# Batch 0 of a fused attention and MLP kernel: unpadded scores, gathered global rows, spare matmuls and a new order of work

## Chip, cores, metric

One core of one Trainium2 chip runs the whole program. The metric is device time in microseconds (us) of one execution, the median of several; lower is better. In one call (a set of kernels run in turn, in the same rounds) the executions of the kernel before lie within 0.2 to 0.7% of each other.

## What is computed

Eight batches of attention over 576 tokens, 8 heads of 64, with a window of 32 tokens to each side and 8 global tokens; then a residual token mixer and a channel MLP with a hidden width of 2048.

```python
mask = (abs(pos[:, None] - pos[None, :]) <= 32) | is_global[:, None] | is_global[None, :]
attn = softmax(where(mask, q @ k.T / 8, -1e9))
x = (attn @ v).transpose(0, 2, 1, 3).reshape(8, 576, 512)

a1 = alpha1 * x + beta1
u = x + lam * einsum("ts,bsd->btd", w_tok, a1)     # token mix
a2 = alpha2 * u + beta2
out = u + lam * (relu(a2 @ w_ch1) @ w_ch2)         # channel MLP
```

## The kernel before

After batch 0 the kernel is one stream of nine groups of MLP matmuls on TensorE, with the attention of the next batch woven in between them. Batch 0 has no MLP to hide behind. Its work is written as a list of short names, the schedule `FIRST`; each name issues a few instructions, and each engine runs its own in the order of the list. `x:3` means that x gets PSUM bank 3.

```python
FIRST = """
i1 kgz qz1 ktz qz0 gb1 pgz gbm:0 gbc cq0 ck0 OH tk0:1 ar1 vez tq0:2 kt0 cq1 ck1 ptz qa0 tq1:3 qb0 tk1:4 qa1
qb1 Vi cq2 ck2 ar2 tq2:5 kt1 tk2:6 qa2 ck3 tt:7 kt2 cq3 kq1 gl0:0 ktt qtt tq3:1 ge0 qb2 gl2:2 qb3 qa3 wi s01:3
...
ad3 we5 tx3:5 W1s ut3 beta1
"""
```

`tk`, `tq` transpose K and Q; `s` are the scores and `e` their exp; `pt`, `pg` multiply them by the mask; `pvx`, `pvy` are probabilities times V; `nx`, `ny` divide by the row sums; `xl` multiplies by alpha1 and lambda; `tm` mixes the tokens; `tx`, `ut` make the MLP's input; `W1s` starts the MLP.

The parts that the change and the argument touch:

```python
    # odd 128-row chunks of V, shifted by 64 rows: two copies by DMA, SBUF to SBUF
    def copy_vo(b):
        ve, vo = Ve[b % 2], Vo[b % 2]
        nc.sync.dma_start(out=vo[0:64], in_=ve[64:128, 0:4])
        nc.sync.dma_start(out=vo[64:128], in_=ve[0:64, 1:5])

    # two heads in one matmul: Q padded with zeros for the other head
    def sc_mm(ps, b, hp, u):
        off = 0
        for t in (3 * u, 3 * u + 1, 3 * u + 2):
            n = 72 if t % 2 == 0 else 64
            mm(ps[:, off : off + 2 * n].rearrange(...), KT[b % 2][:, hp, 64 * t : 64 * t + P], QP[:, hp, :, t, 0:n], True, True)
            off += 2 * n

    # rows of the global tokens picked by one-hot matmuls (batches 0 and 1)
    def glob_mm(ps, b, hp, n):
        for i in range(n):
            for m, st_ in enumerate((KB0, QB0[b])):
                o = ps[:, 16 * i + 8 * m : 16 * i + 8 * m + 8]
                for j in range(4):
                    mm(o, quad(st_, hp + i, j), OH[:, j, :], j == 0, False)
                mm(o, TSB[:, 128 * (hp + i) : 128 * (hp + i) + 128], OH[:, 4 + m, :], False, True)
    ...
    # constants: all issued at the start
    for t_, src in ((LA1, alpha1), (LAM, lam)):
        nc.sync.dma_start(out=t_, in_=src.unsqueeze(0).to_broadcast([P, DM]))
    for r in (64, 0):
        nc.sync.dma_start(out=LB[r : r + 1, :], in_=beta1.unsqueeze(0))
    nc.sync.dma_start(out=abr[0:4, :], in_=beta2.rearrange("(c p) -> c p", p=P))
    nc.sync.dma_start(out=abr[4:8, :], in_=alpha2.rearrange("(c p) -> c p", p=P))
    ...
    nc.sync.dma_start(out=A2, in_=alpha2.unsqueeze(0).to_broadcast([P, DM]))
```

The softmax here doesn't subtract the row's maximum and nothing guards it: scores larger than these inputs give would overflow.

Of the kernel before, what the change touches and what calls it, by code (L numbers as in the profile page):

```python
# [18 lines left out]
D = 64  # L19
# [26 lines left out]
i1 kgz qz1 ktz qz0 gb1 pgz gbm:0 gbc cq0 ck0 OH tk0:1 ar1 vez tq0:2 kt0 cq1 ck1 ptz qa0 tq1:3 qb0 tk1:4 qa1  # L46
qb1 Vi cq2 ck2 ar2 tq2:5 kt1 tk2:6 qa2 ck3 tt:7 kt2 cq3 kq1 gl0:0 ktt qtt tq3:1 ge0 qb2 gl2:2 qb3 qa3 wi s01:3
GM gl1:4 e01 tk3:6 s00:7 ge1 kt3 s02:5 e02 ge2 ab:0 s11:1 s12:3 e00 s10:4 abe gk1:6 e12 pgc mask e11 pt0 gk0:5
e10 fz eg1 pg1 pg0 eg0 q1:2 pt1 s21:7 ra1 s22:0 b1i q0:3 e21 G s20:1 ra0 s31:4 e20 s30:6 rd0 s32:5 e22 beta
pvx0:7 e31 pg2 pvy0:3 nx0 e32 wt2:1 e30 wt1:0 ny0 we2 pg3 q2:4 wt3:5 we1 pt2 q3:7 ra2 we3 wt4:6 LA1 rd2 ra3  # L50
wt0:3 xm0 we4 rd1 pvx2:1 rd3 we0 pvx1:0 xl0 nx2 pvy1:5 pvy2:4 nx1 xl2 rs:2 pt3 xl1 ny2 pvx3:7 re rf ny1 xm2
pvy3:6 tm0:3 ny3 xm1 v1 xm3 tm2:4 ad0 nx3 tm1:5 ru:2 rv ad2 xl3 tx0:6 ad1 tx2:3 ut0 tx1:7 ut2 tm3:4 ut1 wt5:1
ad3 we5 tx3:5 W1s ut3 beta1
# [4 lines left out]
def _consts():  # L58
# [19 lines left out]
    c32[:, 40:44] = 4 * p[:, None] + np.arange(4)[None, :]  # L78
    c32[:, 44] = np.where(p < 64, 512 + p, -1)
    c32[:, 45] = np.where(p >= 64, 448 + p, -1)  # L80
# [22 lines left out]
def kernel(ctx, tc, q, k, v, global_idx, alpha1, beta1, w_tok, alpha2, beta2, w_ch1, w_ch2, lam, out):  # L103
# [34 lines left out]
    OH = T("OH", [P, 6, 8], BF16)  # L138
# [56 lines left out]

    KST = XR[:, 4:8, :].rearrange("p a b -> p (a b)").rearrange("p (h j d) -> p h j d", h=H, j=4)
    QST = XR[:, 8:12, :].rearrange("p a b -> p (a b)").rearrange("p (h j d) -> p h j d", h=H, j=4)
    WTB = HTt[:, 0 : 5 * S].rearrange("p (c s) -> p c s", c=5)
# [50 lines left out]
    def gather_x(i):  # L249
        for a in range(2):  # L250
            nc.vector.tensor_scalar(out=KQX[i][:, a, :], in0=KQG[i], scalar1=C32[:, 30 + a : 31 + a], scalar2=None, op0=ALU.mult)
# [32 lines left out]

    def gk_ev(ps, q0, n):
        nc.scalar.activation(out=EG[:, q0 : q0 + n], in_=ps[:, 0:n], func=AF.Exp, bias=0.0, scale=0.125)
# [12 lines left out]
    def probs_q(hp):  # L299
        e, pg = E[hp % 2], PGQ[hp]  # L300
        p1 = e.ap[0]
        gq_in = bass.AP(e.tensor, e.offset + 64, [p1, [272, 5], [72, 2], [1, 8]])
        gq_m = bass.AP(gqm.tensor, gqm.offset, [gqm.ap[0], [8, 5], [0, 2], [1, 8]])
        for c0 in (64, 96):
            nc.vector.tensor_tensor(out=pg[:, :, c0 : c0 + 16].rearrange("p c (a g) -> p c a g", a=2), in0=gq_in, in1=gq_m, op=ALU.mult)  # L305

    def probs_k(hp):
        e, pt = E[hp % 2], PT[hp % 2]
        p0, p1 = pt.ap[0], e.ap[0]
        for par, n in ((0, 5), (1, 4)):  # L310
            w = 72 if par == 0 else 64
            nc.vector.tensor_tensor(  # L312
                out=bass.AP(pt.tensor, pt.offset + 64 + 128 * par, [p0, [256, n], [1216, 2], [1, 64]]),
                in0=bass.AP(e.tensor, e.offset + 144 * par, [p1, [272, n], [w, 2], [1, 64]]),
# [17 lines left out]
    def sc_exp(ps, hp, u):  # L332
        n = UOFF[u + 1] - UOFF[u]
        nc.scalar.activation(out=E[hp % 2][:, UOFF[u] : UOFF[u + 1]], in_=ps[:, 0:n], func=AF.Exp, bias=0.0, scale=0.125)  # L334

    def sc_unit(b, hp, u):
        def f():
            ps = sc_ps()
            sc_mm(ps, b, hp, u)
            sc_exp(ps, hp, u)  # L340
            if u == 2:
                probs_q(hp)
                probs_k(hp)
# [25 lines left out]
    def pv_mms(b, hp, i, o):  # L369
        par = b % 2  # L370
        gs = slice(128 * i, 128 * i + 128) if i < 4 else (slice(576, 704) if par == 0 else slice(512, 640))
        pt = PT[hp % 2]
# [24 lines left out]
    def xl_eng(b, hp):  # L397
        return nc.vector if (b, hp) in ((0, 3),) else nc.gpsimd
# [16 lines left out]
    def norm_y(ps, b, hp):  # L415
# [3 lines left out]
        norm(ps, rt, 1, 1, r0, r0 + 64, SR[r0 : r0 + 64, (b // 2) % 2, cs].rearrange("p (i a d) -> p i a d", i=1, a=2))  # L419

# [50 lines left out]
    def tok_tile(b, i):  # L471
        par = b % 2

        def f():
            ps = pv_ps()
            cs = slice(64 + 128 * i, 192 + 128 * i)
# [7 lines left out]
    def tok_shared(p):  # L484
        def f():
            ps = pv_ps()
            for s in range(5):
                for par in range(2):
                    l = wt4o[:, 0:64] if s == 4 and par == 1 else wtT[:, s, 0:64]
# [113 lines left out]
    def pair_q(ps, hp, a, copy):  # L603
        ps, r = ps.bitcast(BF16), slice(64 * a, 64 * a + 64)
        copy(
            out=QP[r, hp, a, 0:8, 0:64].rearrange("p t (u j) -> p t u j", j=4),
            in_=ps[r, 0:512].rearrange("p (j t u) -> p t u j", j=4, t=8),
        )

    def tr_pair(b, hp):  # L610
        def f():
# [4 lines left out]
            for a in range(2):  # L616
                pair_q(psq, hp, a, nc.vector.tensor_copy)
# [17 lines left out]

    def tr_tail(b):
# [8 lines left out]
    def glob_mm(ps, b, hp, n):  # L645
        for i in range(n):
            for m, st_ in enumerate((KB0, QB0[b])):
                o = ps[:, 16 * i + 8 * m : 16 * i + 8 * m + 8]
                for j in range(4):
                    mm(o, quad(st_, hp + i, j), OH[:, j, :], j == 0, False)  # L650
                mm(o, TSB[:, 128 * (hp + i) : 128 * (hp + i) + 128], OH[:, 4 + m, :], False, True)

    def glob_ev(ps, hp, n):
        v_ = ps[:, 0 : 16 * n].rearrange("p (i m) -> p i m", m=16)
        for a in range(2):
            r = slice(64 * a, 64 * a + 64)
            k0 = KGP[r, hp, 16 * hp + 8 * a : 16 * hp + 8 * a + 8]
            nc.vector.tensor_copy(out=bass.AP(KGP.tensor, k0.offset, [k0.ap[0], [P + 16, n], [1, 8]]), in_=v_[r, :, 0:8])
            q_, d0 = v_[r, :, 8:16], QP[r, hp, a, 0, 64:72]
            nc.vector.tensor_copy(  # L660
                out=bass.AP(QP.tensor, d0.offset, [d0.ap[0], [2 * NW * 72, n], [144, 5], [1, 8]]),
                in_=bass.AP(q_.tensor, q_.offset, [q_.ap[0], [16, n], [0, 5], [1, 8]]),
            )

    def glob(b, hp):
        def f():
            ps = pv_ps()
            glob_mm(ps, b, hp, 1)
# [413 lines left out]
```

## Time and profile before

| | before |
|---|---|
| time, median of three (range) | 401.21 us (400.45 to 403.22) |
| span of the profiled run | 398.0 us |
| first MLP matmul | 45.97 us |
| scores begin | 14.9 us |
| TensorE idle before the first MLP matmul | 11.6 of 46 us |

The profile is of another execution, of 399.87 us. The span is some 2 us shorter than the time of the same run. The first MLP matmul is where batch 0 hands over to the stream; the prediction calls it T0, and so does this document. T0 says what batch 0 costs, and the span minus T0 says what the rest costs. The lines for all this are in the prediction.

### The profile page before, as it was taken

The page shows a single profiled execution, that of the slowest core. Times are in us where ns is not written, and L with a number is a line of the kernel's source. Part 1 is how long each engine was busy: PE and PEld are TensorE (multiplying, and loading weights), DVE is VectorE, ACT ScalarE, POOL GpSimd, SP SyncE. Part 2 cuts the span into 40 slices and gives each one's busy share as a digit, 9 for nine tenths or more (in the row PEclk, how much of TensorE's full clock was granted, in tenths as well). Part 3 has the DMA queues.
Part 4 walks back from the last instruction along what each step waited for, and adds up shares of the span by engine and source line. Part 5 has one row for each costly group of instructions (what it writes and reads, how often), then busy time and mean ns, then how long its engine had stood idle before and what let it go on. Part 6 is the DMA issues. An engine that isn't in the chain of part 4 may idle for free.

```text
span 398.0 us, 8191 instructions
## 1 busy us (share of the span) xinstructions
PE 376.7 (95%) x3088; PEld 213.5 (54%) x3141; DVE 228.8 (57%) x615; ACT 169.0 (42%) x322; POOL 212.8 (53%) x282
## 2 busy tenths in 40 slices
PE   6668989998999999999999999999999999999996
PEld 3557666554664466546654665466546654444443
DVE  5657786876457656774578467754775564114023
ACT  4644577201870186008700870088108800640720
POOL 8925987447946883687367936874350335000000
PEclk9988999999999999999999999999999999999999
DMA  9999999986998999799959995999331004102002
GB/s 247 196 241 253 216 149 141 127 139 113 153 153 123 153 145 133 101 117 170 130 107 148 134 147 107 140 143 150 94 94 40 2 28 98 49 1 79 28 26 79
DMA packets 161628, 48.68 MB, mean 122 GB/s; under 512 B 147324, under 2 KB 154564, under 8 KB 161590
## 3 DMA queue, kind: packets, MB, share of 16 engines
q0 software_dynamic: 99840, 17.19, 66.0%
q1 hardware_dynamic: 60662, 29.93, 38.8%
q10 hardware_dynamic: 1088, 1.05, 0.8%
q8 instruction: 24, 0.39, 0.4%
q14 instruction: 14, 0.11, 0.1%
HBM read 39.31 MB, written 9.44 MB: 122 GB/s over the span
## 4 chain that ended last, share of the span: by engine, by line
PE 85%; POOL 5%; DVE 4%; DMA 3%; issue 2%; ACT 0%; SPq 0%; POOLq 0%
PE bank L130 84%; DMA Vo<-Ve 2%; POOL Ve L213 1%; PE bank L813 1%; DMA UT<-UB 1%; DVE XR L543 1%; DVE XR L841 1%; DVE OT L542 1%; DVE XR L395 0%; PE bank L595 0%; POOL PGQ L570 0%; POOL Ve L570 0%; DVE PT L312 0%; POOL W L701 0%; POOL PGQ L789 0%
## 5 line engine op out<-in xcount | busy, mean ns | idle before, releaser
L130 PE MATMUL bank<-UT,W 128*128 128x512 bf16 x546 | 152.8, 379 | 2.5 <-DMA UT<-UB 1.1
L130 PE MATMUL bank<-W,HT 128*128 128x512 bf16 (+2 forms) x572 | 138.0, 373 | 1.0 <-issue 0.2
L527 ACT ACTIVATE HT<-bank,bias 128x512 bf16<-128x512 f32 x128 | 87.8, 687 | 52.6 <-PE bank L130 51.8
L334 ACT ACTIVATE E<-bank 128x416 f16<-128x416 f32 (+1 forms) x96 | 47.2, 515 | 122.3 <-PE bank L130 121.5
L130 PEld LDWEIGHTS <-HT 128*128 128x128 bf16 x592 | 53.3, 98 | 52.7 <-issue 1.6
L413 POOL TENSOR_TENSOR XL<-XR,LA 128x384 bf16<-128x384 f32 x31 | 31.3, 1012 | 75.3 <-DVE XR L395 53.8
L130 PEld LDWEIGHTS <-W 128*128 128x128 bf16 x640 | 50.7, 97 | 28.0 <-issue 2.1
L542 DVE TENSOR_TENSOR OT<-bank,LAM 128x512 f32<-128x512 f32 (+2 forms) x37 | 24.9, 674 | 54.8 <-PE bank L130 54.6
L468 POOL TENSOR_TENSOR UB<-XR,A 128x512 bf16<-128x512 f32 x28 | 35.8, 1288 | 23.7 <-DVE XR L463 15.8
L130 PEld LDWEIGHTS <-PT 128*128 128x128 f16 x576 | 33.5, 99 | 22.7 <-DMA Vo<-Ve 3.8
L130 PE MATMUL bank<-RG,G 128*128 128x65 f16 x320 | 43.9, 194 | 1.0 <-DVE RG L356 0.6
L130 PE MATMUL bank<-Ve,PT 128*128 128x65 f16 x320 | 44.0, 196 | 0.1
L130 PE MATMUL bank<-XL,wtT 128*128 128x512 bf16 (+2 forms) x238 | 41.1, 326 | 0.1
L130 PE MATMUL bank<-Vo,PT 128*128 128x65 f16 x256 | 35.6, 194 | 4.6 <-DMA Vo<-Ve 3.6
L130 PEld LDWEIGHTS <-G 128*128 128x128 f16 x320 | 31.2, 98 | 14.3
L213 POOL DMA_DIRECT2D Ve<-in_v_dram x40 | 34.1, 868 | 2.9 <-PE bank L130 2.5
L130 PEld LDWEIGHTS <-KT 128*128 128x128 bf16 x288 | 24.5, 100 | 17.8 <-issue 1.3
L130 PE MATMUL bank<-QP,KT 128*128 128x144 bf16 (+1 forms) x288 | 33.0, 228 | 0.9 <-DVE QP L660 0.6
L395 DVE TENSOR_TENSOR XR<-bank,rd 128x384 f32<-128x384 f32 (+1 forms) x64 | 27.2, 425 | 2.3
L543 DVE TENSOR_TENSOR XR<-OT,XR 128x512 f32<-128x512 f32 (+2 forms) x33 | 27.2, 825 | 1.6
L130 PEld LDWEIGHTS <-wtT 128*128 128x128 bf16 (+1 forms) x240 | 18.6, 99 | 17.6 <-issue 1.7
L305 DVE TENSOR_TENSOR PGQ<-E,gqm 128x80 f16<-128x80 f16 x64 | 10.2, 201 | 30.7 <-ACT E L334 29.5
(137 smaller groups left out, 426.4 us busy)
## 6 DMA issues: line engine op xcount, KB each, us to landing
out_dram<-XR SPq DMA_DIRECT2D x31, 256.0 KB, 2.0
Vo<-Ve SPq DMA_DIRECT2D x16, 260.0 KB, 5.4
W<-in_moe_w_ch_dram POOLq DMA_DIRECT2D x4, 1024.0 KB, 24.3
Ve<-in_v_dram POOLq DMA_DIRECT2D x24, 128.0 KB, 6.7
Kb<-in_k_dram POOLq DMA_DIRECT2D x24, 128.0 KB, 5.2
Qb<-in_q_dram POOLq DMA_DIRECT2D x24, 128.0 KB, 6.2
Ve<-in_v_dram POOLq DMA_DIRECT2D x16, 96.0 KB, 3.8
XR<-in_q_dram ACTq DMA_DIRECT2D x4, 256.0 KB, 3.9
```

The costliest lines, as they stand in the source:

```text
L130: nc.tensor.matmul(out=o, lhsT=l, rhs=r, start=st, stop=sp, skip_group_check=True)
L213: nc.gpsimd.dma_start(out=Ve[b % 2][r0 : r0 + hi - lo, c, :, 0:D], in_=v[b, :, lo:hi, :].rearrange("h p d -> p h d"))
L305: nc.vector.tensor_tensor(out=pg[:, :, c0 : c0 + 16].rearrange("p c (a g) -> p c a g", a=2), in0=gq_in, in1=gq_m, op=ALU.mult)
L334: nc.scalar.activation(out=E[hp % 2][:, UOFF[u] : UOFF[u + 1]], in_=ps[:, 0:n], func=AF.Exp, bias=0.0, scale=0.125)
L395: nc.vector.tensor_tensor(out=xo, in0=pv[:, :, :, 0:64], in1=rb, op=ALU.mult)
L413: xl_eng(b, hp).tensor_tensor(out=XL[b % 2][:, 0:3, cs], in0=XR[:, base : base + 3, cs], in1=lb, op=ALU.mult)
L468: nc.gpsimd.tensor_tensor(out=ub, in0=x, in1=A2, op=ALU.mult)
L527: nc.scalar.activation(out=HT[:, ec, :], in_=st[ec], func=AF.Relu, bias=b_, scale=1.0)
L542: nc.vector.tensor_tensor(out=ot, in0=ps, in1=LAM[:, lo:hi], op=ALU.mult)
L543: nc.vector.tensor_tensor(out=x, in0=ot, in1=x, op=ALU.add)
L813: nc.tensor.transpose(out=ps[0:n, 64 + 128 * t : 192 + 128 * t], in_=WTB[:, t, cols], identity=identb)
L841: nc.vector.tensor_tensor(out=x, in0=ps.rearrange("p (i c) -> p i c", i=4), in1=x, op=ALU.add)
```

## The change

The intent is to shorten batch 0. Odd V chunks come from VectorE instead of the DMA. Scores use the 64 rows of one head, so Q needs no zero padding. The rows of the global tokens come by an indirect DMA (a gather) in place of one-hot matmuls, for batch 1 too. w_tok is loaded in runs of six rows. 29 spare matmuls, whose results nobody reads, are to hold TensorE's clock up in its waits. Constants and batch 1's K and Q are held back until VectorE has written one element (a gate, `gat1`), so that batch 0's data comes first. And the whole list was solved anew; it also lets batch 1's attention start earlier in the stream. The core of the diff:

```diff
 FIRST = """
-i1 kgz qz1 ktz qz0 gb1 pgz gbm:0 gbc cq0 ck0 OH tk0:1 ar1 vez tq0:2 kt0 cq1 ck1 ptz qa0 tq1:3 qb0 tk1:4 qa1
...
+vez kgz ktz pgz gb1 gbm:0 W0 gbc V0 ck0 cq0 ar0 tq0:1 idn gath tk0:2 sp:5 ar1 qv0 ck1 pgc ar2 tk1:3 sp:6 kt1
+cq1 V1 ck2 mask tq1:4 kt0 V2 cq2 tk2:5 qv1 kt2 tq2:6 sp:4 V3 ck3 gx tk3:0 V4 qv2 gt:1 kt3 tt:3 sp:4 ge0 wki
+gte ktt ge1 wi z00:2 qtt cq3 s00:5 z20:4 GM s20:6 z21:0 e001 s21:1 tq3:3 e201 z01:5 sp:1 e200 s01:6 ptz2 qv3
+e210 z11:4 sp:2 e011 voa z10:0 z31:3 e000 gk0:6 v1f gat1 e211 gk1:2 vob eg0 s10:1 e010 pg2 fz s11:6 eg1 pg0
...
+    def sc0_mm(pss, hp, u):
+        off = 0
+        for t in range(5 * u, 5 + 4 * u):
+            n = 72 if t % 2 == 0 else 64
+            for a in range(2):
+                r = slice(64 * a, 64 * a + 64)
+                mm(pss[a][:, off : off + n], KT[0][r, hp, 64 * t : 64 * t + P], Q0[r, hp, t, 0:n], True, True)
+            off += n
...
+    def ld_const():
+        fill(LA1[0:1, 0:1])
+        for t_, src in ((LA1, alpha1), (LAM, lam)):
+            nc.sync.dma_start(out=t_, in_=src.unsqueeze(0).to_broadcast([P, DM]))
+        ... (beta1, beta2, alpha2, as before)
+        for h0 in (0, 4):
+            ld_kq(k, KST, nc.sync, 1, h0, h0 + 4)
+            ld_kq(q, QST, nc.sync, 1, h0, h0 + 4)
...
+    def spare(n):
+        for _ in range(n):
+            mm(banks[7][:, 0:256], identb, C32.bitcast(BF16)[:, 0:256], True, True)
...
+        "voa": lambda: V_.tensor_copy(out=Vo[0][0:64], in_=Ve[0][64:128, 0:4]),
+        "vob": lambda: V_.tensor_copy(out=Vo[0][64:128], in_=Ve[0][0:64, 1:5]),
+        "gat1": ld_const,
+        "gath": lambda: gather(0),
...
-        "LA1": lambda: V_.tensor_tensor(out=LA1, in0=LA1, in1=LAM, op=ALU.mult),
-        "beta": lambda: b0_beta(0),
+        "LA1": lambda: g_.tensor_tensor(out=LA1, in0=LA1, in1=LAM, op=ALU.mult),
+        "beta": lambda: b0_beta(0, g_),
...
-            parts = [(first_attention(1), 18, 95), ([(1.0, bias_mm)], 96, 97), (token_mix(1), 106, 119)]
+            parts = [(first_attention(1), 8, 90), ([(1.0, late_rows), (1.0, bias_mm)], 91, 93), (token_mix(1), 101, 115)]
```

## The prediction

> **What bounds the kernel now.** I read the page's slices first, then the busy-time table by stretch, the waits of the first 46 us, and the timeline of TensorE and of the other engines there.
>
> ```profile
> PE   6668989998999999999999999999999999999996
> PEclk9988999999999999999999999999999999999999
> ```
>
> A digit is a tenth of a slice of 9.95 us. After slice 5 TensorE is full; the kernel is a long MLP stream (nine groups, into which the attention of later batches is woven), preceded by batch 0, which has no MLP to hide behind. The table by stretch puts numbers on it (length, then busy us of PE, weight load, DVE, ACT, POOL, then clock, DMA share, GB/s):
>
> ```profile
> 46.00:100.00 54.00, 50.32 (x500) 29.79 (x507) 38.94 (x109) 21.80 (x45) 37.01 (x44) 1.00 1.56 140
> 100.00:200.00 100.00, 99.10 (x842) 56.30 (x858) 61.37 (x172) 49.92 (x98) 67.74 (x84) 1.00 1.53 136
> 0.00:46.00 46.00, 34.37 (x407) 26.38 (x409) 29.77 (x98) 23.24 (x46) 32.79 (x66) 0.93 1.24 232
> ```
>
> In the first 46 us TensorE is idle 11.6 us; in the next 54 us 3.7 us, and from 100 to 200 us 0.9 us. So what counts is when batch 0 hands over, and that is visible: the first MLP matmul starts at 45.97. Call this T0. The 352.0 us after it (398.0 - 46.0) are TensorE work and should move along one to one.
>
> What fills the 46 us? The waits of TensorE in that stretch (total, times, longest):
>
> ```profile
> PE bank L130 <- DMA Vo<-Ve: 3.6, 1, 3.6
> PE bank L624 <- DMA TSB<-in_q_dram: 2.2, 1, 2.2
> PE bank L595 <- DVE Kb L584: 1.3, 2, 0.6
> PE bank L130 <- DVE KGP L570: 1.2, 1, 1.2
> PE bank L130 <- DVE PT L312: 0.9, 1, 0.9
> ```
>
> The largest is the copy of the odd V chunks by DMA, on the chain of waits as 7.57 us. It does more harm than its length, as two-microsecond windows and two timeline rows show:
>
> ```profile
> 26.00:28.00 2.00, 0.92 (x17) 0.92 (x18) 0.00 (x0) 0.00 (x0) 0.00 (x0) 0.67 1.11 238
> 28.00:30.00 2.00, 2.00 (x24) 1.58 (x22) 1.75 (x8) 0.56 (x1) 0.00 (x0) 0.50 1.11 236
> 30.00:32.00 2.00, 2.00 (x17) 1.49 (x15) 1.64 (x5) 1.59 (x5) 0.79 (x2) 0.50 1.11 237
> 32.00:34.00 2.00, 2.00 (x33) 1.76 (x33) 0.30 (x1) 1.54 (x4) 1.03 (x2) 0.62 1.12 234
> 28.79 0.61 PE L813 MATMUL bank<-C,HT 128*128 128x128 bf16 x4
> 44.76 0.40 PE L813 MATMUL bank<-C,HT 128*128 128x128 bf16 x4
> ```
>
> The granted clock falls to 0.50 after the wait. PV matmuls start 0.055 us apart at 27 to 28 us and 0.030 us apart after 33.5 us. The whole stretch from 27.1 to 33.4, 6.3 us of nearly unbroken TensorE work, ran at half speed. At full speed it is about 3.2 us, so the wait costs 3.6 + 3.1 = 6.7 us.
>
> The clock row deceives at the start: it says full, but the matmuls tell otherwise:
>
> ```profile
> 1.21 4.02 PE L130 MATMUL bank<-KGP 128*128 128x512 bf16 x9 [1.21 <-DVE KGP L570]
> 45.97 2.75 PE L130 MATMUL bank<-UT,W 128*128 128x512 bf16 x11
> ```
>
> Nine take 4.02 us (0.45 each), later eleven of the same shape 2.75 (0.25). Transposes at 6 to 16 us show 0.58 to 0.61 us per four, as in the half-clock stretch. So TensorE also ran cold until about 19 us, though there it mostly waited for others.
>
> **What the Trainium skill says.** (1) "TensorE: Matmul & The Clock Gate", "What's actually happening": the array runs at half clock by default and after an idle window of about 3.4 us, and at full clock after a busy one. The trace agrees: half-speed matmuls at the start, and 0.50 after an idle of 3.65 us. (2) The same page, "Part 4: PE-mode transpose", says that transposes don't count as busy for this. That fits the cold 6 to 16 us, in which they are most of the work, and it is a reason for the spare ordinary matmuls. (3) "VectorE: DVE Perf Modes", "The perf-mode tier table": a 16-bit copy within SBUF runs at four elements a cycle, 693 ns for 2048. The trace has such a copy, 64x576 in 0.23 us. (4) "SBUF — State Buffer", "Who interferes with whom": VectorE and GpSimd exclude each other on one port pair. The trace agrees: the mask product takes 0.82 us for two alone, and 1.95 at 35.5 us beside GpSimd's XL product.
>
> **The change part by part.**
>
> *Odd V chunks.* Removed: the DMA copy. Added: two VectorE copies of 2080 elements each, estimated at 0.7 us from (3). They need V, whose last load landed near 19.6 us (issued at 12.6, 7.0 to land); V is now issued piece by piece, the last at my estimate of 11 us, so the copies should be done near 18 us, before PV needs them. Gain: the 3.6 us wait.
>
> *Spare matmuls.* 29 of 256 columns, about 0.11 us each warm: 3.1 us, placed where TensorE waits, so nearly free. They prevent the half clock: 3.1 us. Warm early work adds perhaps 0.5 us, since VectorE and ScalarE set the pace there.
>
> *Scores on unpadded Q.* A Q pair is one 128x512 copy in place of two 64x512: saves 0.58 to 0.68 us four times, 2.5 us of VectorE and ScalarE. Score matmuls go from 36 to 72 at half the columns, TensorE about equal. The exp goes from 12 pieces (416, 400, 416 columns) to 16 (344, 272). From rows of 0.383 us for 256 columns and 0.531 for 416, a piece costs some 0.15 us fixed plus 0.0009 per column, so ScalarE gets 4 x 0.15 = 0.6 us more. The global-key scores halve from 16 to 8 matmuls, 1.3 us saved of 2.6.
>
> *Gathered globals.* Removed: 40 one-hot matmuls (about 2 us in all around 13.6 to 16 us) and 16 small VectorE copies (0.16 to 0.23 us, 3 us). Added: two gathers on GpSimd (1.07 + 0.99 us as at 49.5 us), 3 to 8 us until they land, two products, two fp32 transposes, five copies, about 2 us in sequence. Gathered at 6 to 8 us, landed near 11 to 14, scores begin near 14 instead of 14.9. The tail of K and Q now goes ahead of everything in its queue, so the 2.2 us wait should go. The same gather serves batch 1: its 40 one-hot matmuls (1.6 us of TensorE after T0, at about 0.40 us a pair) and their copies go too. A sum of five short matmuls returns, so 1.3 us net.
>
> *w_tok.* 30 transposes before and after, five evictions of 0.64 instead of six, larger pieces in the DMA. About 0.6 us of ScalarE; the 0.93 us of late row sums leaves batch 0.
>
> *Balance.* Three norms go to ScalarE, XL of two head pairs to VectorE. With durations as above, adding up from a start of useful data near 13 us: ScalarE still has some 19 us to do (exp 6.5, globals 0.8, evictions of tails and globals 1.3, RG 1.5, w_tok 3.2, norms 3.0, row sum 0.6, UT 2.8) and VectorE some 21 us (PT 3.3, PGQ 1.2, G and GM 2.1, norms and their reciprocals 4.1, RG 1.2, XL 2.1, adds 2.7, V copies 1.4, rest 2.5). So no schedule hands over before 32 to 34 us; dependencies and the shared port cost 2 to 3 more.
>
> *Sum.* From before: 46.0 - 3.6 - 3.1 - 2.2 (tail, of which half is only moved: -1.1 counted) - 1.5 (later one-hots, warmer start, better order) = 36.7. From the balance: 34 + 2.5 = 36.5. I take T0 = 36.5, so 9.5 us earlier, plus 1.3 us from batch 1: 401.2 - 10.8 = 390.4.
>
> **The rivals.** *W1 arrives late.* The second half of W1, issued at 15.4, took 21.9 us to land, so about 37.3, well before 46 but after my T0. The new split by rows also makes the first matmuls need both halves. Against it: its issue moves some 2 us earlier, V and w_tok ahead of it too, and batch 1's K and Q are held back by a gate. For it: constants and those loads then share the same 20 to 35 us. If W1 lands at 38, the time is 392; if at 40, 394.
>
> *W2 arrives late.* It must now wait until batch 0 is done with the buffers borrowed inside it, so it is issued near 35 us in place of 20.6. It then took at most 26.8 us under full load. Its first use was 24.4 us after T0, so about 61. Likely safe (35 + 22 = 57 or less), else 1 to 4 us lost, and a delay of batch 2's loads that follow in the queue; time 391 to 394.
>
> *VectorE and GpSimd become the bound.* Both carry some 30 us of work before T0. If the exclusion seen at 35.5 us is common, T0 is 39 and the time 393. *The clock stays low*, since spare matmuls are too few: 2 to 3 us more, 393.
>
> **Range and chances.** One mechanism (DMA wait and half clock, 6.7 us) I trust; the rest, some 4 us, may be halved, or improved on by a better order to T0 = 33. That gives 386.5 to 395. The limit of 2% is 393.2, so it takes two of the rivals, or W1 badly late, to miss it: faster 0.74, same 0.23, slower 0.03.
>
> **What would show it.** Right: no wait for Vo; clock 1.00 at 20 to 34 us, and PV matmuls 0.030 us apart; first MLP matmul near 36.5; 350 to 351 us after it. Wrong: a TensorE wait ended by a DMA into W, by KQG, or idle time of over 5 us between T0 and T0 + 54 us; a granted clock of 0.5 after 20 us; or a first MLP matmul after 40 us, which would be engine work that I have undercounted.

## The result

| | before | after | predicted |
|---|---|---|---|
| time, median (range) | 401.42 us (400.45 to 403.22) | 397.60 us (397.25 to 397.81) | 390.4 (386.5 to 395) |
| span of the profiled run | 398.0 us | 395.6 us | |
| T0 | 45.97 us | 44.28 us | 36.5 |
| span after T0 | 352.0 us | 351.3 us | about 350.7 |
| scores begin | 14.9 us | 16.44 us | near 14 |

The ratio is 0.9899, with a 95% interval from 0.9863 to 0.9935. Ratios here are the mean time of one kernel's runs over that of the other's runs of the same rounds, so not quite the ratio of the medians in the tables. Executions over 1.5% slower than the fastest of the same kernel are left out of the means. The changed kernel is 1.0% faster: within 2%, and outside the predicted range. Nearly the whole miss is in T0.

The slices of the page after, a tenth of busy time per digit, a slice being 9.9 us:

```profile
PE   5767799999999999999999999999999999999996
PEclk9696989999999999999999999999999999999999
```

TensorE is full from the sixth slice on; the fourth to sixth are 7, 7 and 9, where they were 8, 9 and 8. The clock is at 6 in two slices, the second (9.9 to 19.8 us) and the fourth (29.7 to 39.6 us). The waits of TensorE in the first 100 us name one cause (engine, what waited, what it waited for; us in total, times, longest):

```profile
PE bank L899 <- DMA abr<-in_moe_alpha_dram: 4.8, 1, 4.8
PE bank L633 <- DVE Kb L622: 2.8, 2, 2.4
PE bank L128 <- DVE E L937: 2.5, 1, 2.5
PE bank L633 <- DVE QP L643: 2.2, 1, 2.2
```

There is no wait for Vo any more. In its place TensorE waits 4.8 us for `abr`, 4 KB of alpha2 and beta2. The same view for all engines shows two more waits; the longest is GpSimd's, for `LAM`, the lambda vector on 128 partitions:

```profile
POOL XL L855 <- DMA LAM<-in_moe_lam_dram: 6.5, 1, 6.5
DVE b2f L902 <- PE bank L899: 4.1, 1, 4.1
```

VectorE stood for 4.1 us too, at its copy of the transpose that TensorE couldn't do without `abr`.

The timelines of VectorE, SyncE's queue, GpSimd and TensorE tell how (start, length, engine, line, operation; in brackets the idle time before it and what ended it):

```profile
19.40 0.75 DVE L921 COPY Vo<-Ve 64x2080 f16<-64x2080 f16 x1
20.10 0.06 DVE L608 MEMSET LA<- 1x1 f32 x1
20.19 0.92 DVE L922 COPY Vo<-Ve 64x2080 f16<-64x2080 f16 x1
...
20.57 0.43 SPq L730 DMA_DIRECT2D LAM<-in_moe_lam_dram  x1
21.97 0.29 SPq L734 DMA_DIRECT2D abr<-in_moe_alpha_dram  x1
...
31.49 1.25 POOL L855 TENSOR_TENSOR XL<-UB,LAM 1x512 bf16<-1x512 f32 x1 [6.54 <-DMA LAM<-in_moe_lam_dram]
...
32.29 0.24 PE L899 MATMUL bank<-ident,abr 8*128 8x8 f32 x1 [4.75 <-DMA abr<-in_moe_alpha_dram]
...
44.28 2.10 PE L128 MATMUL bank<-UT,W 128*128 128x512 bf16 x9
```

The gate is the 0.06 us memset at 20.10, issued between the two V copies. Only then do the constants start, and 10.2 us after its issue (21.97 to 32.2) the last of those that TensorE needs could be used. Meanwhile TensorE stands in order at a small transpose of `abr`, which nothing before the MLP's input needs. The idle time then costs a second time, as the two-microsecond windows show (length, busy us of PE, weight load, DVE, ACT, POOL, then clock, DMA share, GB/s):

```profile
28.00:30.00 2.00, 0.00 (x0) 0.00 (x0) 0.49 (x3) 1.01 (x5) 0.00 (x0) 0.91 1.05 260
30.00:32.00 2.00, 0.00 (x0) 0.00 (x0) 0.00 (x0) 0.00 (x0) 0.51 (x1) 0.50 1.03 336
32.00:34.00 2.00, 1.71 (x5) 0.75 (x6) 1.42 (x4) 0.00 (x0) 1.92 (x2) 0.50 1.07 364
34.00:36.00 2.00, 2.00 (x25) 1.57 (x24) 1.93 (x4) 0.58 (x1) 1.92 (x3) 0.50 1.06 376
```

By 30 us the clock is at 0.50, and it stays there until 36.5, with TensorE busy without a break from 32.3. That is 4.2 us of work at half speed, 2.1 us lost. So the change took away a stall of 3.6 + 3.1 = 6.7 us, as predicted, and put another of 4.8 + 2.1 = 6.9 us of the same kind in its place.

### The profile page after: what moved, and what is told of

Read it like the earlier page. It is cut to its first block, busy times and chain, and to the rows that moved or that the text cites. A ratio compares the mean times of both kernels' runs of the same rounds, so it can differ in the third digit from the quotient of the medians.

```text
span 395.6 us, 8168 instructions
## 1 busy us (share of the span) xinstructions
PE 376.0 (95%) x3116; PEld 210.4 (53%) x3116; DVE 230.0 (58%) x589; ACT 169.0 (43%) x338; POOL 214.7 (54%) x277
## 3 DMA queue, kind: packets, MB, share of 16 engines
q10 hardware_dynamic: 1232, 1.12, 0.9%
## 4 chain that ended last, share of the span: by engine, by line
PE 90%; DMA 5%; DVE 3%; issue 0%; SPq 0%; ACT 0%; ACTq 0%; DVEq 0%
PE bank L128 88%; DMA abr<-in_moe_alpha_dram 3%; DMA KQG<-in_k_dram,hidx 2%; DMA C<-c_np 1%; DVE OT L622 1%; PE bank L633 0%; DVE QP L643 0%; DVE QP L249 0%; ACT W L362 0%; PE bank L893 0%; DVE XR L581 0%; DVE OT L580 0%; SPq L730 0%; DVE XR L889 0%; PE bank L695 0%
## 5 line engine op out<-in xcount | busy, mean ns | idle before, releaser
L128 PE MATMUL bank<-UT,W 128*128 128x512 bf16 x576 | 160.5, 381 | 0.0
L128 PE MATMUL bank<-W,HT 128*128 128x512 bf16 (+2 forms) x592 | 140.3, 373 | 0.0
L366 ACT ACTIVATE E<-bank 128x416 f16<-128x416 f32 (+1 forms) x84 | 41.7, 514 | 115.7 <-PE bank L128 114.9
L128 PEld LDWEIGHTS <-HT 128*128 128x128 bf16 (+1 forms) x610 | 54.4, 98 | 53.4 <-issue 1.6
L128 PEld LDWEIGHTS <-W 128*128 128x128 bf16 (+1 forms) x658 | 51.6, 98 | 25.5 <-issue 0.3
L580 DVE TENSOR_TENSOR OT<-bank,LAM 128x512 f32<-128x512 f32 (+2 forms) x37 | 24.9, 674 | 54.2 <-PE bank L128 53.9
L128 PE MATMUL bank<-Ve,PT 128*128 128x65 f16 x300 | 41.9, 196 | 0.0
L128 PEld LDWEIGHTS <-KT 128*128 128x128 bf16 (+1 forms) x324 | 23.5, 101 | 18.3 <-issue 1.5
L214 POOL DMA_DIRECT2D Qb<-in_q_dram x30 | 27.0, 898 | 4.5 <-DMA W<-in_moe_w_ch_dram 4.5
L128 PE MATMUL bank<-QP,KT 128*128 128x144 bf16 (+1 forms) x252 | 28.9, 224 | 0.0
L214 POOL DMA_DIRECT2D Kb<-in_k_dram x30 | 27.0, 900 | 1.7 <-DMA W<-in_moe_w_ch_dram 1.6
```

The lines of the kernel that those rows point to most:

```text
L128: nc.tensor.matmul(out=o, lhsT=l, rhs=r, start=st, stop=sp, skip_group_check=True)
L214: nc.gpsimd.dma_start(out=dst[0:n, c, :].rearrange("p (h d) -> p h d", d=D), in_=src[b, :, c * P : c * P + n, :].rearrange("h p d -> p h d"))
L366: nc.scalar.activation(out=eb(b, hp)[:, UOFF[u] : UOFF[u + 1]], in_=ps[:, 0:n], func=AF.Exp, bias=0.0, scale=0.125)
L580: nc.vector.tensor_tensor(out=ot, in0=ps, in1=LAM[:, lo:hi], op=ALU.mult)
```

## The experiments

Theory A: the wait for the constants, with the half clock after it, is what eats the gain. Theory B: VectorE and GpSimd hinder each other and set T0. Theory S: the start is late, because of the gather. (The expectations also have a C, that constants loaded at the start push K and Q back, and a V, that VectorE's own row of work sets T0.) And a further question: does an earlier T0 shorten the program at all? Eighteen kernels ran. All gave results within the tolerance of the reference. T0 and the span are those of one profiled run each, so differences under 0.5 us there mean little (the changed kernel's two profiles, the first and e6, have T0 44.28 and 44.55).

| run | built on, with | us | ratio (95%) | T0 | span after T0 |
|---|---|---|---|---|---|
| e1_const_early | changed, constants ungated at the start | 392.58 | 0.9831 (0.9803 to 0.9860) | 42.14 | 348.6 |
| e2_abr_early | changed, only abr early | 396.08 | 0.9916 (0.9893 to 0.9939) | 44.54 | 348.9 |
| e3_before_vo_dve | before, batch 0's odd V by VectorE | 400.17 | 1.0027 (0.9995 to 1.0059) | 41.56 | 353.8 |
| e4_before_spares | before, 36 spare matmuls | 400.29 | 1.0014 (0.9989 to 1.0038) | 44.29 | 353.9 |
| e5_const_mid | changed, constants gated at 11 us | 393.63 | 0.9853 (0.9836 to 0.9869) | 42.40 | 348.7 |
| e6_changed_again | changed, unaltered | 397.23 | 0.9924 (0.9905 to 0.9943) | 44.55 | 351.3 |
| e7_const_mid_late_weave | e5, batch 1 woven as before | 395.14 | 0.9883 (0.9849 to 0.9916) | 41.72 | 351.0 |
| e8_before_vo_both | e3, batch 1's odd V by VectorE too | 397.21 | 0.9934 (0.9917 to 0.9950) | 42.52 | 352.9 |
| e9_no_gather_wait | e1, plain rows for the gather | 394.49 | 0.9831 (0.9787 to 0.9875) | slow run | |
| e10_pool_order | e1, GpSimd's products earlier | 394.31 | 0.9844 (0.9823 to 0.9866) | 44.78 | 347.9 |
| e11_more_spares | e1, 28 more spares | 392.44 | 0.9803 (0.9781 to 0.9825) | 42.79 | 347.9 |
| e12_combined | e1, e10, e11, A2 later | 394.62 | 0.9860 (0.9834 to 0.9886) | 44.69 | 347.9 |
| e13_xl_vector | e1, all XL on VectorE | 392.00 | 0.9773 (0.9736 to 0.9810) | 41.92 | 348.6 |
| e14_no_spares | e1, no spares | 393.12 | 0.9805 (0.9753 to 0.9856) | 41.67 | 350.2 |
| e15_plain_rows | e1, plain rows on GpSimd's queue | 393.51 | 0.9829 (0.9788 to 0.9870) | 42.63 | 348.5 |
| e16_la1_vector | e1, alpha1 product on VectorE | 392.32 | 0.9796 (0.9744 to 0.9848) | 41.84 | 348.5 |
| e17_vector_ballast | e16, three more products on VectorE (2.25 us) | 392.56 | 0.9800 (0.9760 to 0.9839) | 42.68 | 348.2 |
| e18_norms_scalar | e16, two norms on ScalarE | 392.24 | 0.9829 (0.9768 to 0.9890) | 41.90 | 347.9 |

### The constants (e1, e2, e5, e6)

**e1_const_early.**

```diff
     nc.sync.dma_start(out=C16, in_=...)
+    (the loads of LA1, LAM, LB, abr, A2, moved here)
     def ld_const():
-        fill(LA1[0:1, 0:1])
-        (those loads)
+        fill(XR[0:1, 4, 0:1])        # gate for batch 1's K and Q alone
```

> Changed kernel, but the constants (alpha, lambda, beta and the small transposed ones) are loaded at the start again, as in the kernel before; only batch 1's K and Q stay behind the gate. Theory A (the gated constants land behind W1, which stops TensorE 4.8 us at the alpha/beta transpose and GpSimd 6.5 us at lambda, and costs half the clock after): both waits go, the clock stays 1.00 from 26 to 37 us, the first MLP matmul comes near 37.5 instead of 44.3, time 391. Rival B (VectorE and GpSimd carry too much work before the handover anyway): first MLP matmul near 42, time 395 to 396. Rival C (the 0.8 MB of constants push K and Q back at the start): waits go, but scores begin 2 us later than in the changed kernel, time 393.

392.58 us, ratio 0.9831. Both waits are gone and the clock is 1.00 from 28 us on, but T0 came only 2.1 us earlier, not by the 6.9 us of the stall. Two things in its trace stand against the gain; how much of the rest each took was not isolated. The constants now share the DMA with batch 0's first loads: the gather lands in 9.8 us instead of 8.1, and scores begin at 18.2 us, 1.8 us later, as rival C expected. And on VectorE and GpSimd, side by side:

```profile
25.16 0.82 DVE L331 TENSOR_TENSOR PT<-E,mask 128x640 f16<-128x640 f16 x2
...
28.11 2.70 DVE L331 TENSOR_TENSOR PT<-E,mask 128x640 f16<-128x640 f16 x2
...
28.04 1.28 POOL L945 TENSOR_TENSOR LA<-LA,LAM 128x512 f32<-128x512 f32 x1
```

The two mask products took 2.70 us beside GpSimd's products; at 25.16 us two of the same take 0.82. The prediction cited the Trainium skill for this exclusion; this is a larger instance than the 1.95 us that it quoted. T0 came where rival B put it (near 42 us), and the time near rival C's 393, for the gain after T0.

**e2_abr_early.** Only the two `abr` loads moved to the start.

> Changed kernel, only the two 2 KB loads that the alpha/beta transpose needs are put at the start; lambda and the other constants stay behind the gate. If the transpose that stands in TensorE's queue is the whole loss, the 4.8 us wait goes and the first MLP matmul is near 37.5, time 391. If lambda is just as late for GpSimd (theory A in full), GpSimd still starts its first scaled product at 34 us, TensorE waits there instead, and the first MLP matmul is at 42 to 44, time 395 to 397.5.

396.08 us. This run tells the two waits apart. TensorE no longer waits for `abr`, yet T0 is unchanged, since it runs on only to the next thing that needs lambda, through GpSimd:

```profile
PE bank L128 <- POOL XL L445: 6.2, 1, 6.2
```

The stall was two deep. What the list of waits shows is the first, not the only one.

**e5_const_mid and e6_changed_again.** In e5 a gate of their own releases the constants at about 11 us, after the mask and ahead of W1. e6 is the changed kernel, unaltered, as a control.

```diff
-cq1 V1 ck2 mask tq1:4
+cq1 V1 ck2 mask gat0 tq1:4          # gat0: fill(LA1[0:1, 0:1]) and the constants' loads
```

> Changed kernel, with a gate of their own for the constants: they are issued once VectorE is past the mask (near 11 us), so after K and Q have landed and ahead of W1, instead of near 20 us. If the late constants are what the changed kernel lost (theory A) and the early ones pushed K, Q and the gather back (C), then both waits go and scores begin at 16.4 as in the changed kernel, not at 18.2: first MLP matmul near 40, ratio to the kernel before 0.976 to 0.980 (about 390.5). If theory B holds (engines), first MLP matmul stays near 42, ratio 0.983 as in the run with early constants.

> The changed kernel itself, unaltered, on the same chip as the others: 0.990 of the kernel before, as measured.

e5 has 0.9853 and e6 0.9924, with intervals apart: the later gate alone costs 0.7% in the same rounds. In e5 scores begin at 15.7 us, so the start is not pushed back as in e1, but TensorE then waits 2.0 us for GpSimd's fill of `PT`, and T0 is the same 42.4. Theory A is right as to direction: without the late constants T0 comes about 2 us sooner, and 2.6 us less follow it. It isn't the whole gap of 7.8 us.

### Does an earlier T0 shorten the program? (e3, e4, e8, e7)

**e3_before_vo_dve** does one part of the change alone, in the kernel before. (The copy by DMA also held back batch 1's K and Q in their queue; a gate of their own now makes them start about where they did.)

```diff
     def b1_kq():
-        copy_vo(0)
+        "voa": lambda: V_.tensor_copy(out=Vo[0][0:64], in_=Ve[0][64:128, 0:4]),
+        "vob": lambda: V_.tensor_copy(out=Vo[0][64:128], in_=Ve[0][0:64, 1:5]), ...
```

> Kernel before, with only one part of the change: the odd V chunks are copied by VectorE instead of by DMA (batch 1's K and Q loads are gated to start where they did). By the prediction this removes the 3.6 us wait and the 3.1 us of half clock: time 394.7, clock 1.00 from 26 to 34 us, first MLP matmul near 39.3. Rival: the two copies (0.75 and 0.92 us) delay masks and PV on VectorE, or another wait takes the place: time 397 to 399.

**e4_before_spares** puts 36 spare matmuls ahead of the first probabilities times V, in the kernel before.

> Kernel before, with 36 spare matmuls of 256 columns (3.9 us at full clock) put ahead of the first PV matmuls, so that TensorE is busy through the 3.6 us wait for the copied V chunks; the wait stays. If half the loss of that wait is the clock, as the prediction has it, the stretch of 27 to 33 us runs at full clock: 3.1 us less, time 398.3. Rival: the stretch is not bound by TensorE, or the clock falls anyway: time 401 to 402.

Neither changed the time: 1.0027 and 1.0014. But T0 moved, by 4.4 and 1.7 us. A wait that took some of it back stands in the timelines of TensorE, first e3, then e4:

```profile
63.03 0.20 PE L130 MATMUL bank<-Vo,PT 128*128 128x65 f16 x1 [1.69 <-DMA Vo<-Ve]
```

```profile
65.32 0.20 PE L130 MATMUL bank<-Vo,PT 128*128 128x65 f16 x1 [1.26 <-DMA Vo<-Ve]
```

This is batch 1's own odd-V copy by DMA. In the kernel before it is issued here and first used here:

```profile
56.85 0.47 SPq L1002 DMA_DIRECT2D Vo<-Ve  x1
57.41 0.56 SPq L1003 DMA_DIRECT2D Vo<-Ve  x1
...
65.59 0.19 PE L130 MATMUL bank<-Vo,PT 128*128 128x65 f16 x1
```

Nothing waited for it there, since batch 0 was slow enough. The copy waits for batch 1's V, whose five loads GpSimd issues at 41.0 to 45.2 us; SyncE's queue stands 25.6 us at it. In e3 the same loads are issued 4.4 us sooner (36.6 to 40.8), but they take up to 16.2 us to land instead of 13.1, and so the copy is issued at 55.50 instead of 56.85, only 1.35 us sooner. TensorE is there sooner, and waits. What slows V's loads was not isolated. This accounts for a part only: the profiled run of e3 was the fastest of its four (397.38 us, against 400.1 to 402.1), and its span is 2.6 us under the span before, so of the 4.4 us at T0 its trace shows 1.8 swallowed. Where the other three executions lost the rest is in no trace.

**e8_before_vo_both** makes batch 1's copy by VectorE too.

> Kernel before, with the odd V chunks of batch 0 and of batch 1 copied by VectorE. In the run with batch 0's alone, the first MLP matmul came 4.4 us earlier but the time didn't fall, and TensorE waited 1.7 us at 61.3 us for batch 1's DMA copy, which landed at 63.0, near where the kernel before used it (65.6). If that transfer is what holds the kernel before in place, removing it lets the 4.4 us through: ratio 0.988 to 0.991 (about 395.5). If something else takes them back (V itself, W2, batch 2's transposes), ratio 0.997 to 1.003.

397.21 us, 0.9934: now 2.6 of the 3.5 us that T0 gained come through (span 395.4 against 398.0). With nothing of the change but odd V by VectorE, for batches 0 and 1, the kernel before is as fast as the changed kernel: 0.9934 against 0.9924 for e6, in the same rounds.

**e7_const_mid_late_weave** is e5 with batch 1's attention woven in as in the kernel before.

```diff
-parts = [(first_attention(1), 8, 90), ([(1.0, late_rows), (1.0, bias_mm)], 91, 93), (token_mix(1), 101, 115)]
+parts = [(first_attention(1), 18, 95), ([(1.0, late_rows), (1.0, bias_mm)], 96, 98), (token_mix(1), 106, 119)]
```

> The kernel with constants by a gate of their own, and batch 1's attention woven in as late as in the kernel before (from MLP item 18 instead of 8). If the wait of TensorE for batch 1's first transposed Q after the handover (1.2 to 2.2 us, and half clock after it in the changed kernel) costs time by itself, it goes and 1 to 2.5 us are gained against the same kernel with the early weave. If the stream is held elsewhere, no difference within 0.5 us.

The time after T0 rises from 348.7 to 351.0 us: the earlier weave is worth about 2.3 us, which the prediction didn't count. What is then left against the 352.0 us of before is 1.0 us, near the 1.3 us that the prediction gave to batch 1's one-hot matmuls; that part was not isolated.

### Where do the remaining 42 us come from? (e9 to e18)

**e9_no_gather_wait**, wrong: the gather lands in tiles that nobody reads, and plain loads of 128 rows, first in SyncE's queue, feed the products.

> Wrong result on purpose. The kernel with early constants, in which the gather of batch 0's global rows still runs but into tiles that nobody reads; the rows used are the first 128 of K and Q, loaded plainly at the start. It takes away only the wait for the gather (2.9 us of TensorE, landing 9.8 us after issue). If that wait is what makes scores begin at 18.2 instead of the 14 us that the prediction took, scores begin near 15.3 and the first MLP matmul comes 2 to 3 us earlier than 42.1, ratio 0.976. If another part of the start (V, Q copies, the half clock) or of GpSimd holds it, the gain is under 1 us, ratio 0.981 or more.

Inconclusive. The plain loads delayed K itself (TensorE then waited 4.3 us for a cast of K), the four runs spread from 391.87 to 398.23 us, and the profiled one counts as slow. **e15_plain_rows** is the same test with the plain loads on GpSimd's queue, behind the tails of K and Q.

```diff
     ld_tail(q, TSB, g_, 0, 64)
+    g_.dma_start(out=KQG[0], in_=kf[0:P, :])       # gather(0) itself goes to tiles nobody reads
+    g_.dma_start(out=KQG[1], in_=qf[0:P, :])
```

> Wrong on purpose: the kernel with ungated constants in which batch 0's gather lands in tiles that nobody reads, and two plain loads of rows 0 to 127, issued on GpSimd's queue right after the tails, feed the products instead. The waits for the gather (landing 9.8 us, TensorE idle or cold until 18.2 us) go. If the gather's landing sets the handover: scores begin 2 to 4 us sooner and the handover comes 1.5 to 3 us sooner, ratio 0.976 to 0.979. Rival, that K, Q and their casts and transposes bind just as late or that VectorE's work swallows the gain: scores begin up to 2 us sooner, handover within 0.7 us of 42.1, ratio 0.981 to 0.985.

(It takes the wrong rows as global ones; the result still passed the tolerance.) The scores' matmuls, by the tile view of e1 and then of e15 (count, shortest, median and longest ns, first and last start):

```profile
L128 PE MATMUL bank<-W,KT x72: 191/208/252, 18.2 to 24.7; 64*128 64x72 bf16 x40, 64*128 64x64 bf16 x32
```

```profile
L128 PE MATMUL bank<-W,KT x72: 189/245/252, 13.7 to 24.5; 64*128 64x72 bf16 x40, 64*128 64x64 bf16 x32
```

They begin 4.5 us sooner and end at the same time; T0 is 42.63. So a sooner start did not move T0 by itself, and theory S isn't supported. But the run isn't a clean test, since it has new losses between. Two products on VectorE, 0.86 us together in e1, took 3.26 (the second 2.84 of them):

```profile
15.28 3.26 DVE L852 TENSOR_SCALAR GM<-EG,C 128x576 f16<-128x576 f16 x2
```

TensorE waited 1.43 us for the VectorE copy behind them, and its clock was at 0.50 from 15 to 27 us. VectorE's V copy starts at 19.8 us (21.1 in e1), and V's last load, 6.6 us from issue to landing, is on the chain of waits of e15. A sooner start without these losses didn't run.

**e10_pool_order**, **e11_more_spares**, **e12_combined.** e10 puts GpSimd's LA1 and beta products ahead of its fills, so that they no longer stand beside the mask product. e11 has 28 more spares (`sp:6` to `sp:20`, `sp:4` to `sp:8`, and ten more before the gather's transposes). e12 joins both and issues A2 after batch 1's K and Q.

> The kernel with early constants, with two GpSimd products (alpha times lambda, beta times lambda) moved ahead of its zero fills of QP, and batch 1's fills put last. In the run with early constants they ran from 26.7 to 29.3 us and the VectorE mask product beside them took 2.70 us instead of 0.82. If the two engines' exclusion there is on the path to the handover (my third rival), that product falls to 0.8 to 1.9 us and the first MLP matmul comes 1 to 2 us earlier than 42.1: ratio 0.979. If not, no change: 0.983.

> The kernel with early constants, with 28 more spare matmuls in the waits between 6 and 16 us (20, 8 and 10 in place of 6, 4 and none). If the half clock from 11 to 22 us is due to idle TensorE there, it stays at full clock; what that is worth at the handover shows how much of the start is TensorE's: 0.5 to 1.5 us if the score stage is paced by TensorE (ratio 0.980), nothing if ScalarE and VectorE pace it (0.983).

> Early constants (without the copy of alpha2, which goes behind the gate), GpSimd order and spares together. If the gains add: first MLP matmul near 39, ratio 0.974 to 0.978, faster than the kernel before by over 2%. If they overlap, 0.980 to 0.983.

e10: the mask products fell from 2.70 to 1.12 us, but the loss moved. Beside the GpSimd products in their new place, from 21.3 to 24.6 us, VectorE's V copies took 0.94 and 1.64 us (0.75 and 0.92 in e1) and the PGQ products behind them 1.26 instead of 0.31; another PGQ, just ahead of the mask products, took 1.25. TensorE had a wait of 2.5 us, from 22.4 to 24.9 us. The profile names no releaser for it, but the slow PGQ ended at 24.79, 0.1 us before it; T0 went to 44.78. e11: the clock is 0.97 in the mean from 12 to 20 us and 1.00 from 20 to 28, T0 is no earlier (though the clock then fell to 0.50 from 33 to 36 us, after a wait of 1.57 us), and the ratio is the same as e1's within the intervals. e12 has e10's loss.

**e14_no_spares** takes all 29 spares out of e1.

> The kernel with ungated constants, all 29 spare matmuls taken out; right results. If the spares matter as predicted (3.1 us of half clock prevented): the granted clock falls to 0.5 for some stretch after 20 us, the handover comes 1.5 to 3 us later, ratio 0.987 to 0.991. Rival, that the clock holds by the real work and VectorE and GpSimd set the pace, so half clock costs little: ratio within 0.003 of 0.983.

T0 is 41.67, as early as with them. The expected fall of the clock column to 0.5 did not show, but the column is no witness here; a window and a timeline row of TensorE of this run:

```profile
16.00:20.00 4.00, 2.66 (x46) 2.02 (x45) 3.30 (x9) 2.85 (x10) 3.89 (x11) 1.00 1.64 185
```

```profile
18.55 0.61 PE L633 MATMUL bank<-C,Kb 128*128 128x128 bf16 x4
```

The column says 1.00, but four transposes take 0.61 us, as in every stretch at half clock (0.40 at full). Matmuls of this run are 0.06 us apart until 25.2 us and 0.03 us from then on: TensorE was cold from the start to 25.2 us, and T0 didn't suffer. After that, with no wait of over 0.7 us, the clock stayed up without spares. So with the constants' stall gone, the spares buy nothing at T0, though they are a part of the change that the prediction gave 3.1 us to. (The time, 393.12 us, is about 1 us above e13's and e16's, but the intervals overlap.)

**e13_xl_vector** moves batch 0's XL products from GpSimd to VectorE, and **e16_la1_vector** moves the product of alpha1 and lambda back to VectorE.

```diff
# e13
-        return nc.vector if (b, hp) in ((0, 1), (0, 3)) else nc.gpsimd
+        return nc.vector if b == 0 else nc.gpsimd
# e16
-        "LA1": lambda: g_.tensor_tensor(...)
+        "LA1": lambda: V_.tensor_tensor(...)
```

> The kernel with ungated constants (e1: 392.6 us, ratio 0.983, first MLP matmul at 42.1 us), and batch 0's four XL products all on VectorE (two were on GpSimd). Theory B, that VectorE and GpSimd shut each other out when both run two-input products (the VectorE mask product took 2.70 us at 28.11 us beside GpSimd's, 0.82 alone): VectorE's products shrink to 0.4 to 0.9 us each, the handover comes 1 to 2 us sooner, ratio 0.979 to 0.981. Rival, that VectorE is simply full by then: the 2 us of XL work that it takes over cost more than the exclusion did, the handover stays or comes up to 1.5 us later, ratio 0.983 to 0.987.

> The kernel with ungated constants, and the one product of alpha1 and lambda (128x512) moved from GpSimd back to VectorE, where the kernel before had it. If the exclusion costs what the mask product shows (2.70 us against 0.82): that product shortens by over 1 us, and the handover comes 0.5 to 1 us sooner, ratio 0.981 to 0.983. Rival, the contention only moves to the next pair of products, as in the run that put this product earlier: handover the same or up to 1.5 us later, ratio 0.983 to 0.987.

Both have a lower ratio than e1's, and T0 moved by 0.2 to 0.3 us. They were run at other times. e16 shows why freeing one product doesn't help. VectorE, TensorE, and then TensorE's windows of 1 us:

```profile
27.08 0.82 DVE L331 TENSOR_TENSOR PT<-E,mask 128x640 f16<-128x640 f16 x2
30.02 1.88 DVE L324 TENSOR_TENSOR PGQ<-W,gqm 128x80 f16<-128x80 f16 x2
...
31.95 0.53 PE L128 MATMUL bank<-Ve,PGQ 128*128 128x130 f16 x5 [1.46 <-DVE PGQ L324]
```

```profile
33.00:34.00 1.00, 1.00 (x12) 1.00 (x10) 0.93 (x4) 0.24 (x2) 1.00 (x2) 0.50 1.07 369
34.00:35.00 1.00, 1.00 (x12) 1.00 (x11) 0.61 (x2) 0.67 (x4) 1.00 (x2) 0.50 1.08 380
```

The mask product is back at 0.82 us, so the exclusion is real. But the next pair of small products on VectorE, 0.3 us when alone, now took 1.88 beside GpSimd's XL products. TensorE waited 1.46 us for it, and its clock was at 0.50 for the next 3 us. From there TensorE had no wait of over 0.5 us until T0. (So waits far shorter than the idle window of about 3.4 us that the prediction cites were followed by half clock: 1.46 us here, and in the changed kernel the clock fell some 2 us into the wait for `abr`. A wait of 1.56 us in e1 was not. The measurements decide; what else it depends on was not tested.)

**e17_vector_ballast** and **e18_norms_scalar** load and relieve VectorE alone, on e16.

```diff
# e17
+        "bal": lambda: [V_.tensor_tensor(out=BAL, in0=mask, in1=mask, op=ALU.mult) for _ in range(3)],
-... q1:6 nx0
+... q1:6 bal nx0
# e18
-                f"nx{h}": lambda h=h: norm_x(hb[f"pvx{h}"], 0, h),
+                f"nx{h}": lambda h=h: norm_xa(...) if h < 2 else norm_x(...),   # six ScalarE activations
# and b2f, a2c copied by nc.scalar
```

> The kernel with ungated constants and the alpha1 product back on VectorE (first MLP matmul at 41.84 us, 353.0 us gone by... span 390.3), with three extra VectorE products of 128x576 fp16 into a tile that nobody reads, at about 28 us; right results. Theory V, that VectorE's own row of work from its first V copy (20.07 us) to the handover sets the handover: the three (about 0.7 us each, 2.1 us) move it one to one, first MLP matmul at 43.5 to 44.0 us, ratio 0.984 to 0.987. Rival, that VectorE's full look is other engines' delays spread out: it takes the three in its stride, handover within 0.7 us of 41.84, ratio within 0.002 of 0.98.

> The same base, with two of VectorE's normalizations (head pairs 0 and 1, 0.56 us each) and the two small alpha and beta copies (0.31 us together) moved to ScalarE, which is busy only 13.4 of the 21.8 us after 20 us; right results. Theory V: VectorE is relieved of some 1.3 us and the handover comes 0.8 to 1.3 us sooner, at 40.5 to 41.0 us, ratio 0.976 to 0.979. Rival, a chain through TensorE, ScalarE and GpSimd binds: handover within 0.4 us of 41.84, or later since the six small ScalarE activations of a norm take longer than one VectorE product, ratio 0.979 to 0.984.

The ballast of 2.25 us moved T0 by 0.84 us. But it also changed what came behind it, the small products that took 1.88 us in e16:

```profile
28.28 2.25 DVE L945 TENSOR_TENSOR BAL<-mask 128x576 f16<-128x576 f16 x3
...
32.05 0.85 DVE L325 TENSOR_TENSOR PGQ<-W,gqm 128x80 f16<-128x80 f16 x2
```

In all VectorE's busy time between 20 us and T0 grew by 0.94 us (19.29 to 20.23), close to the 0.84 us by which T0 moved. Taking 2.5 us of its busy time away (19.29 to 16.80 us) moved T0 by 0.06 us. VectorE then waits for ScalarE instead:

```profile
30.04 0.30 DVE L388 SCALAR_TENSOR_TENSOR RG<-bank,RG 32x130 f16<-32x130 f32 x1 [1.61 <-ACT RG L384]
```

So theory V is neither shown nor refuted: the load that really came on top moved T0 nearly one for one, and the relief went into a wait for another engine. Ten kernels without the constants' stall and without e10's order (e1, e5, e7, e11, e13 to e18) have T0 between 41.67 and 42.79 us. This fits a tight schedule in which engines take turns and none alone decides, but what holds T0 near 42 us was not shown, and which single rearrangement would lower it is left open. The half clock of some 3 us near 32 to 36 us isn't it: e11, e16, e17 and e18 have it, e1, e13 and e14 don't, with the same T0. Keeping GpSimd's products away from all of VectorE's at once didn't run.

**A version that beats both kernels.** e1, e11, e13 and e16 have medians from 392.0 to 392.6 us, which these runs don't tell apart: 1.7 to 2.3% under the kernel before by their ratios. e1 is the simplest of them, the constants' loads without their gate.

## Why the prediction was wrong

**First step that failed: the balance of T0 (13 + 21 + 2.5 = 36.5).** VectorE's books of the same stretch, after and e1:

```profile
13.00:44.28 31.28, 23.95 (x371) 19.20 (x370) 23.34 (x63) 17.30 (x48) 23.12 (x36) 0.79 1.21 205
```

```profile
13.00:42.14 29.14, 23.11 (x371) 18.39 (x370) 23.94 (x64) 17.34 (x48) 25.04 (x39) 0.85 1.49 220
```

VectorE did 23.3 us of work where 21 were predicted, and stood idle for 31.28 - 23.34 = 7.9 us where 2.5 were allowed ("dependencies and the shared port cost 2 to 3 more"). That is the 7.8 us of the miss: 2.3 of more work and 5.4 of more idle time (2.34 and 5.44 before rounding). Of the idle time 4.1 us are the wait behind the transpose of `abr`. With the constants early, idle time is 5.2 us, so they explain 2.7 us of it, and the other 2.7 us over the allowance stay. In e1 most idle time lies before 20 us (3.6 us), where VectorE waits for the gather (3.5 us, 2.9 of them in this stretch). e15 took that wait away and T0 did not move, but it brought losses of its own. After 20 us VectorE is busy for 20.50 of 22.14 us. By an estimate most of e1's extra work (23.94 against 21) is stretching beside GpSimd: three pairs of products took 2.70, 0.85 and 1.11 us instead of 0.82, 0.31 and 0.82, 2.7 us in all. So the sum of rows, each taken as it is when alone, was too small, and the start too late; how much of T0 each is worth stays open, since e13 to e16 and e18 took pieces away and T0 stayed.

**Within it: the constants.** The prediction saw that the gate held the constants and batch 1's loads back, and asked only what this would do to W1. It didn't ask who reads the constants: a transpose on TensorE and a product on GpSimd, both in the middle of batch 0. The rivals W1 and W2 were read from landing times, and neither came about; the same reading, done for `abr` and `LAM`, could have found this one. Every removed wait has this rival, another wait that takes its place, and the list of rivals had it only for W1 and W2.

**Second step that failed: "The 352.0 us after it (398.0 - 46.0) are TensorE work and should move along one to one."** For the kernel before this is false, as e3 and e4 show: T0 alone gained nothing in time, and a part went into a wait for batch 1's copy of odd V, near 63 to 65 us; with that copy on VectorE (e8), 2.6 of 3.5 us come through. For the changed kernel it happened to hold, since V of batch 1 is loaded ahead of W2 there and its copies are issued at 48.0 and 48.6 us. The predicted 350.7 us were met at 351.3 by two errors that cancel: the earlier weave, uncounted, brought about 2.3 us (e7), and a new wait of 2.2 us for `QP`, with the clock at 0.53 and 0.61 in the 4 us from 50 us on (by an estimate from these, 1.7 us of work lost), took it back. In e1 that wait is 1.2 us, the clock stays at 1.00, and 348.6 us remain: 2.7 us less, as 1.0 + 1.7 would give.

**The 6.7 us "I trust".** The Vo wait went, and VectorE's copies took 0.75 and 0.92 us against an estimate of 0.7 each. The half clock didn't go: it followed the wait to its new place. The mechanism was right; the error was to count it as removed with one of its causes, and at its full length. In the kernel before, without the Vo wait and with the clock at 1.00 from 24 to 44 us, T0 gained 4.4 us (e3), and 36 spares alone gained 1.7 of the 3.1 us (e4). In e1 the spares gain nothing at T0: e14 does without them.

**Terms that came out.** No wait for the tails of K and Q is left. Scores began at 16.44 us instead of 14: the gather landed after 8.1 us, at the edge of "3 to 8". What this start is worth at T0 is open: e15 started sooner and gained nothing. Of the rivals, the one in which VectorE and GpSimd become the bound (T0 39, time 393) was the nearest: right as to the exclusion, 3 us short on T0 in e1, and near on the time (392.6) because of the gain after T0. Two of the prediction's signs of being wrong came: half clock after 20 us, and a first MLP matmul after 40 us.

**Lines misread.** The prediction has a copy of 64x576 in 0.23 us; these copies take 0.43 to 0.45 us, and 0.23 is the part that lies on the chain of waits. The page's figure was the better guide: copies of 2080 elements took 0.70 us in e8. ScalarE's listed items add up to 19.7 us, not 19. V copies were done at 21.1 us after the change, not near 18.

## What to carry to other kernels

When loads are held back by a gate, list for each of them its first reader on every engine, with the landing time beside it; a small constant that an engine meets early, in order, can stall it as a large tensor does (here 2 KB of `abr` took 10.2 us until used, 256 KB of `LAM` 10.8). A gain at one point of a stream counts only up to the next transfer that doesn't land sooner for it (in e3 the copy came 1.35 us sooner for 4.4), so look for the slack of that transfer before adding the gain to the sum. A product's time when alone isn't its time beside another engine: add up rows from a stretch in which both run. And in a schedule where engines take turns, count idle time from a measured schedule of the same kind instead of allowing a small sum for it: here it was a fifth to a quarter of the stretch.

## What the Trainium skill lacked or had wrong

- "DMA: Bandwidth & Descriptors", section "Anatomy of one DMA — SWDGE (gpsimd) path": it fits a transfer that GpSimd issues as about 2.0 us fixed plus the bytes over 436 GB/s. For the gather of 128 rows of 64 fp32 (32 KB), issued by GpSimd while other loads are in flight, that gives an estimate of 2.1 us; it took 8.1 us after the change and 9.8 in e1. Among its latencies the page has a remark on memory under load, but no measured time of a whole transfer in traffic. The same goes for loads from SyncE's queue, which the fit doesn't cover: 2 KB of `abr` took 10.2 us. Whether it was W1 that held them up was not isolated.
- "SBUF — State Buffer", section "Who interferes with whom": right that VectorE products of two SBUF inputs contend with GpSimd instructions that read SBUF. What it lacks is the size of it in a real pair of rows, 0.82 to 2.70 us for two products and 0.3 to 1.88 us for two small ones, and that moving one GpSimd product out of the way handed the loss to other VectorE instructions (e10, e16).
- "TensorE: Matmul & The Clock Gate", section "Seeing it yourself": it warns that the recorded clock events are unreliable on trn2, which these runs bear out; what it lacks is the form seen here, a clock row that stands at full speed from the start until the first recorded change. It stood at 1.00 for the whole start of e14, where four transposes took 0.61 us instead of 0.40 until 25.2 us, and in the kernel before, where the prediction noted it. The spacing of equal matmuls is the better witness.
